# Gated linear and softmax attention: query features turned by VectorE in 32 by 32 blocks, numerators on sixteen tiles of TensorE, value tiles by way of DRAM

## The chip, the cores and the metric

The kernel runs on one core of one Trainium2 chip. The metric is the device time of one execution in microseconds; the median of several runs is given. Engines are named as in the profile: PE (TensorE, with PEld for its weight loads), DVE (VectorE), ACT (ScalarE), POOL (GpSimd), SP (SyncE, which issues most DMAs here). "Line L538" is a line of the kernel before, unless it is said to be of the changed one; the two have other line numbers.

## The reference, cut

Two attentions over the same input, S=2048 tokens, D=448, H=16 heads of Dh=28, mixed by a gate for each token.

```python
def A(x, wqkv, w_phi, wo):                       # hedgehog, linear
    q, k, v = split_heads(x @ wqkv)
    pq = einsum("bhsd,hdf->bhsf", q, w_phi)      # and pk from k
    phi_q = concatenate([softmax(pq), softmax(-pq)], -1)   # 56 features a head; phi_k too
    kv  = einsum("bhsf,bhsd->bhfd", phi_k, v)
    z   = einsum("bhsf->bhf", phi_k)
    num = einsum("bhqf,bhfd->bhqd", phi_q, kv)
    den = einsum("bhqf,bhf->bhq", phi_q, z)[..., None] + 1e-6
    return merge_heads(num / den) @ wo
def B(x, wqkv, wo):                              # softmax attention
    q, k, v = split_heads(x @ wqkv)
    return merge_heads(softmax(q @ k.T * Dh**-0.5) @ v) @ wo
g = sigmoid((x * gate_w).sum(-1, keepdims=True))
return g * A(x) + (1 - g) * B(x)
```

## The kernel before

**Number format.** Projections are made of fp32r products. Weights and x are split into a high and a low part (XH, XL), and a projection of 128 tokens takes, for each of four blocks of rows, two products of XH (with the high and the low part of the weights), and for three of them one of XL: 11 matmuls of 448 columns, called passes here (`tok_major`, L135; `run`, L117).

**Stages.** The text of the kernel is one list of calls, and each engine does its instructions in the order of that list, so the order of the calls sets the order of the work.

1. To 62 us: queries and keys of B (`proj_qk`, tiles pqk), written to DRAM.
2. 62 to 173 us, loop `t`=0..15 over tiles of 128 tokens: the features of A's keys (pk, `features1`, `features2`), A's values (pva, `value_a`), what is left of B's projections, and `kv_add` (L489), which adds two tiles of keys to the sum pkv, as 64 small products on four 128 by 32 tiles of TensorE.
3. 173 to 253 us, loop `q`=0..15: the features of A's queries, then their use. This is what is changed.
4. To 311 us: the rest of A's outputs (poa), with some value tiles of B (pvb, `value_b`, L753); to 335 us the rest of B's values.
5. 335 to 985 us: the attention loop of B (scores st, exponentials p, products pv), then the end.

**One tile of queries.** `tok_major` makes the product pq. ScalarE copies it out of PSUM (pcq, L451). VectorE takes largest and smallest of each head (extq, L453 and L454), GpSimd subtracts (L457; the second half L459, on VectorE for tiles 1 to 10, else on GpSimd), ScalarE takes the exponential in place in one of four feature tiles (feat0 to feat3, L462), VectorE sums and inverts (fsumq, L469 and L470), GpSimd multiplies (L471). The exponentials stand in a list, `exps`; `take_exps(1)` issues all but the newest, so one is left pending until the next tile. `turn` (L525) then transposes the tile on TensorE, in eight 128 by 128 transposes into PSUM tiles pft (L535), which ScalarE copies to SBUF as fT (L538). For each two tiles, `numer` (L541) multiplies fT by KV, the sum of the keys, in 32 products of 256 columns on eight 64 by 32 tiles (pn, L549).

**Behind a numerator.** `normalize1` copies it out (oU) and sends the row of denominators through DRAM, `normalize2` adds and inverts them on VectorE (dena, L418, L419) and sends them out again, `normalize3` multiplies (L430), `normalize4` splits into high and low part (oTa, L438, L439). `out_a` (L593) multiplies by wo in 12 passes (poa), `out_a2` multiplies by the gate on ScalarE (ga, L601) and stores.

**Units.** The softmax of B needs a bound of each row's maximum. It is made in 56 small pieces that are placed wherever there is room, called units (`mx_unit`, L269): four matmuls of 28 rows into two tiles of two banks each (pmb, pmd, L295), a relu of pmd on ScalarE (rl, L298), and two reductions over pmb and rl on VectorE (L300). `tick` calls a unit between two passes when a count of passes has come to the next number of a list, `pace["at"]`. In stage 2 a unit stands at the start of every second tile, and one or two more by `tick`; in stage 3 and 4 one to each tile from q=11 on.

**PSUM.** Eight banks: before q=20, three for the single-bank tiles (`ps_s`), among them pq, pft, pn and poa, four for pmb and pmd, one for pkv. From q=2 on, every fourth `ps_s` tile takes pkv's place (`turn4`). At q=20 the pool is closed and opened again with another split (`psn`).

## Time and profile before

| | |
|---|---|
| median of 3 runs | 1003.8 us (1003.21 to 1003.91) |
| the profiled execution's own time | 1003.26 us |
| its span | 1001.5 us |
| instructions | 18001 |
| PE busy | 994.9 us (99%) |
| ACT busy | 807.8 us (81%) |
| DVE busy | 659.8 us (66%) |
| POOL busy | 240.0 us (24%) |

Busy times are over the whole span. A timeline row gives the start in microseconds from the span's start, the length, the engine, the line, the operation, the tile written and the tiles read, and how many instructions the row holds; behind it, in brackets, a wait and its releaser. Matmuls are pipelined, so a row's own length overlaps the next one's, and prices are read from start to start. A row of the groups gives the line, the engine, the operation, the count, the busy time and the mean in ns, and then the idle time before them with what ended it.

### The profile page before, as it was taken

What the parts mean: (1) busy time and instruction counts of PE and PEld (TensorE: products, weight loads), DVE (VectorE), ACT (ScalarE), POOL (GpSimd) and SP (SyncE); (2) the same over time, 40 slices, a digit from 0 to 9 for tenths busy, and PEclk for the clock granted to TensorE, in tenths of its full rate; (3) what the DMA queues carried; (4) which work ended last, traced back from release to release, by engine and by line L of the source; (5) the groups of instructions that cost most, each with busy time, mean ns of one, the idle gap of its engine ahead of it and who ended that gap; (6) DMA issues with size and microseconds to landing.
All of it is one profiled execution on the core that took longest, in us unless ns stands there. A gap on an engine that the chain in (4) does not pass through costs nothing.

```text
span 1001.5 us, 18001 instructions
## 1 busy us (share of the span) xinstructions
PE 994.9 (99%) x6472; PEld 557.7 (56%) x6472; DVE 659.8 (66%) x1335; ACT 807.8 (81%) x1532; POOL 240.0 (24%) x222
## 2 busy tenths in 40 slices
PE   9999999999999999999999999999999999999998
PEld 8878878888777533333333333333334444455656
DVE  6467676887645588888888788888886544444202
ACT  5445555567855899999999999999999999979672
POOL 1265455678625211110120100102011011101010
PEclk9999999999999999999999999999999999999999
DMA  8977312312235832332525324443233264216231
GB/s 290 313 238 218 104 66 76 146 46 80 91 114 129 174 87 54 88 82 70 108 58 105 81 51 141 88 101 94 59 88 75 66 125 117 53 38 147 64 105 56
DMA packets 68353, 107.28 MB, mean 107 GB/s; under 512 B 18520, under 2 KB 28424, under 8 KB 68264
## 3 DMA queue, kind: packets, MB, share of 16 engines
q1 hardware_dynamic: 68264, 106.13, 39.0%
q8 instruction: 51, 0.84, 0.4%
q14 instruction: 38, 0.31, 0.1%
HBM read 73.44 MB, written 31.45 MB: 105 GB/s over the span
## 4 chain that ended last, share of the span: by engine, by line
PE 99%; DVE 0%; ACT 0%; issue 0%; POOL 0%; POOLq 0%; ACTq 0%
PE st L991 28%; PE pv L1092 25%; PE pm L332 9%; PE pqk L117 6%; PE poa L117 4%; PE pva L135 4%; PE pk L135 4%; PE pq L117 4%; PE pob L117 3%; PE pmb L295 2%; PE pvb L135 2%; PE pft L535 2%; PE pvb L117 1%; PE pqk L688 1%; PE pn L549 1%; PE pkv L489 1%
## 5 line engine op out<-in xcount | busy, mean ns | idle before, releaser
L994 ACT ACTIVATE p<-st 128x512 f32<-128x512 f32 x1020 | 527.9, 642 | 25.8 <-PE st L991 25.7
L343 DVE TENSOR_REDUCE part<-pm 128x1 f32<-128x512 f32 x450 | 287.6, 686 | 151.1 <-PE pm L332 151.1
L991 PE MATMUL st<-qst,kst 128*128 128x512 f32 x1020 | 301.3, 423 | 0.8 <-ACT vb L753 0.5
L1092 PE MATMUL pv<-p,vb 128*32 128x512 f32 x2048 | 263.6, 602 | 0.0
L991 PEld LDWEIGHTS st<-qst,kst 128*128 128x128 f32 x1020 | 168.8, 188 | 100.1 <-ACT p L994 45.0
L336 ACT ACTIVATE rl<-pm 128x512 f32<-128x512 f32 x200 | 124.7, 624 | 14.6 <-PE pm L332 13.0
L332 PEld LDWEIGHTS pm<-kc,qc 28*128 28x128 f32 x800 | 38.3, 181 | 167.7 <-issue 100.6
L430 POOL TENSOR_TENSOR oUb<-oUb,rsb 128x512 f32<-128x512 f32 x15 | 19.3, 1286 | 459.3 <-DMA rsb<-rdb 332.5
L340 DVE CUSTOM_DVE_ANT_0 rl<-pm,rl 128x512 f32<-128x512 f32 x150 | 102.2, 681 | 0.0
L332 PE MATMUL pm<-kc,qc 28*128 28x512 f32 x800 | 101.2, 495 | 0.0
L1092 PEld LDWEIGHTS pv<-p,vb 128*32 128x32 f32 x2048 | 47.4, 108 | 95.4 <-issue 88.7
L300 DVE CUSTOM_DVE_ANT_0 rl<-pmb,rl 128x512 f32<-128x512 f32 x112 | 72.1, 681 | 40.4 <-ACT rl L298 40.3
L298 ACT ACTIVATE rl<-pmd 128x1024 f32<-128x1024 f32 x56 | 57.6, 1028 | 17.0 <-PE pmd L295 9.4
L117 PE MATMUL pqk<-XH,wB 128*128 128x512 f32 x192 | 59.3, 397 | 0.0
L625 ACT CAST ev<-pqk 128x512 fp32r<-128x512 f32 x28 | 16.1, 588 | 37.9 <-PE pqk L117 28.8
L117 PE MATMUL poa<-woA_s,oTa 128*128 128x448 f32 x180 | 40.7, 375 | 0.0
L117 PEld LDWEIGHTS pqk<-XH,wB 128*128 128x128 f32 x192 | 35.4, 188 | 8.5 <-issue 1.5
L1107 DVE SCALAR_TENSOR_TENSOR acc<-pob,gate,acc 128x448 f32<-128x448 f32 x12 | 8.2, 681 | 47.1 <-PE pob L117 47.1
L135 PE MATMUL pva<-wvA_s,XH 128*128 128x450 f32 x128 | 38.6, 375 | 0.0
L135 PE MATMUL pk<-wkA_s,XH 128*128 128x448 f32 x128 | 37.5, 374 | 0.0
L626 DVE TENSOR_TENSOR ev<-pqk,ev 128x512 fp32r<-128x512 f32 x28 | 19.0, 690 | 28.0 <-ACT ev L625 27.9
L117 PE MATMUL pq<-wqA_s,XH 128*128 128x448 f32 x128 | 37.3, 374 | 0.0
(172 smaller groups left out, 1163.3 us busy)
## 6 DMA issues: line engine op xcount, KB each, us to landing
qkd<-ev SPq DMA_DIRECT2D x28, 512.0 KB
qst<-qkd SPq DMA_DIRECT2D x64, 224.0 KB
kst<-qkd SPq DMA_DIRECT2D x64, 224.0 KB
od<-oTb SPq DMA_DIRECT2D x48, 112.0 KB
rsa<-rda SPq DMA_DIRECT2D x8, 512.0 KB
rsb<-rdb SPq DMA_DIRECT2D x15, 256.0 KB
kc<-qkd SPq DMA_DIRECT2D x64, 56.0 KB
gad<-ga SPq DMA_DIRECT2D x16, 224.0 KB
```

Source lines behind the costliest of these rows:

```text
L117: nc.tensor.matmul(dst, l, r, start=i == 0, stop=i == len(todo) - 1)
L135: nc.tensor.matmul(dst[:, :n], l, r, start=i == 0, stop=i == len(todo) - 1, skip_group_check=True)
L295: nc.tensor.matmul((pb if j < 2 else pd)[:, j % 2, :], qc[js, qt * P:(qt + 1) * P], kc[js, :], start=True, stop=True, tile_position=(32 * ...
L298: nc.scalar.activation(rl, pd, AF.Relu)
L300: nc.vector.tensor_tensor_reduce(rl[:, i, :], pb[:, i, :], rl[:, i, :], 1.0, LOWEST, ALU.add, ALU.max, part[:, col + i:col + i + 1])
L332: nc.tensor.matmul(pm[j], mxs[("qc", gq)][js, qt * P:(qt + 1) * P], mxs[("kc", g, kb)][js, :], start=True, stop=True, tile_position=(32 * ...
L336: nc.scalar.activation(rl, pm[kb], AF.Relu if kb < 3 else AF.Copy)
L340: nc.vector.tensor_tensor_reduce(r, pm[j], r, 1.0, LOWEST, ALU.add, ALU.max, part[:, col + j:col + j + 1])
L343: nc.vector.tensor_reduce(part[:, col + j:col + j + 1], pm[j], AX.X, ALU.max)
L991: nc.tensor.matmul(st, kst_of[(gq // NQ, kt // 4)][:, j, (kt % 4) * P:(kt % 4 + 1) * P], qst_of[gq][:, j, :], start=True, stop=True)
L994: nc.scalar.activation(p, st, AF.Exp, scale=SCALE)
L1092: nc.tensor.matmul(pv[32 * j:32 * j + 32, :], vb[kt // 8][:, kt % 8, 4 * g + j, :], pt[j], start=kt == 0, stop=kt == NT - 1, tile_position ...
```

## The change

1. **Feature tiles.** A tile of features is [128, 32, 32] instead of [128, 16, 64]: each half head has 28 features and four zeros of its own.
2. **`turn`.** One VectorE transpose of 1024 columns, which turns each block of 32 by 32 by itself, instead of eight TensorE transposes and the copies out of PSUM. Four tiles make one fT.
3. **`numer`.** Over four tiles of tokens at once, 128 products of 128 columns on sixteen 32 by 32 tiles, each sum made of two (b=0, 1). Four numerators instead of eight. Since a block is turned by itself, row block a of the array holds tokens 32a to 32a+31 of each of the four tiles, so the outputs, the gate and `ga_d` are laid out anew: `out_a(n, a)` is for the 128 tokens of row block a, the gate goes through DRAM into that order (`g_d`, z_s), and `load_acc` reads in four DMAs.
4. **KV** has eight blocks instead of four, from eight transposes (`kv_out`).
5. **Engines.** The second subtraction of `features1` is on GpSimd for all queries; `normalize1` copies two tiles at once; the first low part of `normalize4` is on VectorE. No exponential of a query is left pending.
6. **Values of B.** Ten value tiles (`EARLY`) instead of three are made in stage 3 (one at q=17), stored to `v_d` in DRAM and loaded later (`load_early`).
7. **Units.** 30 in stage 2, by `tick` every 418/30 passes; one each at q=0 and 1; none from q=2 to 18; 20 from q=19 on, by `tick` within the passes, with a list of four SBUF buffers (`rls`).
8. **PSUM and SBUF.** The pool is closed and opened again at q=4 instead of q=20. The first stacks of the attention loop (qst0, kst0) take wqA's place and are loaded from q=21.

The same functions and the loop, cut to what differs most:

```diff
 def features1(pp, nm, eng):
-        nc.gpsimd.tensor_sub(f[:, :, :DH], pc,
+        nc.gpsimd.tensor_sub(f[:, 0::2, :DH], pc,
                              ext[:, 0, :].unsqueeze(2).to_broadcast([P, H, DH]))
-        eng.tensor_sub(f[:, :, DH:2 * DH],
+        eng.tensor_sub(f[:, 1::2, :DH],
                        ext[:, 1, :].unsqueeze(2).to_broadcast([P, H, DH]), pc)
...
 def turn(u):
-        for a, b, p in zip(cut, cut[1:], pt):
-            for n in range(a, b):
-                nc.tensor.transpose(p[:, (n - a) * P:(n - a + 1) * P],
-                                    f[:, n * P:(n + 1) * P], ident)
-        for a, b, p in zip(cut, cut[1:], pt):
-            nc.scalar.copy(fT_of[tb][:, a:b, tl * P:(tl + 1) * P],
-                           p[:, :(b - a) * P].rearrange("p (n q) -> p n q", q=P))
+        if u % 4 == 0:
+            fT_of[u // 4] = ta.tile([P, 4, 2 * H, 32], F32, tag="fT", name=f"fT{u // 4}", bufs=1)
+        nc.vector.transpose(fT_of[u // 4][:, u % 4].rearrange("p h t -> p (h t)"),
+                            fq.pop(u).rearrange("p h f -> p (h f)"))
...
 def numer(n):
-        for gp in range(2):
-            for r in range(2):
-                for c in range(4):
-                    nc.tensor.matmul(pn[r][32 * c:32 * c + 32, gp * 256:gp * 256 + 256],
-                                     KV[rows, 32 * h:32 * h + 32], fT_of[tb][rows, n, :],
-                                     start=True, stop=True, tile_position=(64 * r, 32 * c),
-                                     skip_group_check=True)
-        num[tb] = normalize1(ta, pn, f"a{tb}", 2)
+        pn = [ps_mx(f"pn{n}_{i}", False) for i in range(2)] if n else pn_next
+        for g in range(NG):
+            for b in range(2):
+                for a in range(4):
+                    for c in range(4):
+                        rows, k = slice(32 * a, 32 * a + DH), 2 * g + b
+                        nc.tensor.matmul(pn[a // 2][32 * c:32 * c + 32, a % 2, g * P:(g + 1) * P],
+                                         KV[rows, k // 4, k % 4 * P + 32 * c:k % 4 * P + 32 * c + 32],
+                                         fT_of[n][rows, :, 2 * (4 * g + c) + b, :],
+                                         start=b == 0, stop=b == 1, tile_position=(32 * a, 32 * c),
+                                         skip_group_check=True)
...
 stage 2, for t in range(NT):
-        if t < NT and t % 2 == 0:
-            mx_unit()
-            passes = (55 if t < NT - 4 else 44) + (4 if t >= 4 else 0)
-            pace["n"] = 4 if t >= 4 else 0
-            pace["at"] = [passes // 3, 2 * passes // 3] if t <= 10 else [passes // 2]
+    pace.update(n=0, at=[j * 418 // 30 for j in range(30)])       # once, ahead of the loop
...
 stages 3 and 4, for q in range(NT + 11):
+    VALUE = {2: 0, 3: 1, 4: 2, 5: 3, 6: 4, 7: 5, 8: 6, 9: 8, 10: 9, 17: 10, 22: 7}
+        if q == NT + 3:
+            pace.update(n=0, at=[14, 21, 27, 43, 50, 65, 72, 79, 86, 93, 100, 106, 112, 118, 124, 130, 136, 141, 146, 150])
+        for u in ((), (q - 3, q - 2), (q - 2,), (q - 2,))[(q - 2) % 4]:
+            if 0 <= u < NT:
+                turn(u)
...
+        if q in VALUE:
+            value_b(VALUE[q], tick if q > NT + 2 else None)
...
+        take_exps()
+        if q % 4 == 2 and 6 <= q <= NT + 2:
+            numer(n4)
```

What stands on TensorE before, in the query stage behind the product of tile 11 (pq11) and ahead of that of tile 12: a unit (pmb28, pmd28), the numerator of tiles 6 and 7 (pn3), an output (poa0) and the turn of tile 8 (pft8).

```order
L295 MATMUL pmb28_2543<-kp0_3_750,qp1_1_907 128x512 x2
L295 MATMUL pmd28_2544<-kp0_3_750,qp1_1_907 128x512 x2
L549 MATMUL pn3_0_2553<-fT3_2449,KV_2053 32x256 x4
L549 MATMUL pn3_1_2554<-fT3_2449,KV_2053 32x256 x4
L549 MATMUL pn3_0_2553<-fT3_2449,KV_2053 32x256 x4
L549 MATMUL pn3_1_2554<-fT3_2449,KV_2053 32x256 x4
L117 MATMUL poa0_2583<-woA_s_1874,oTa0_0_2494 128x448 x6
L117 MATMUL poa0_2583<-woA_s_1874,oTa0_1_2497 128x448 x6
L535 MATMUL pft8_0_2600<-ident_76,feat0_464 128x128 x4
L535 MATMUL pft8_4_2601<-ident_76,feat0_464 128x128 x4
```

And of the changed kernel, from the last passes of pq14 on: an output, and the first rows of the numerator of tiles 8 to 11 (pn2), which reads the third fT.

```order
L116 MATMUL pq14_2966<-wqA_s_661,XL_94 128x448
L116 MATMUL pq14_2966<-wqA_s_661,XH_93 128x448 x2
L116 MATMUL poa0_3_2995<-woA_s_1947,oTa0_1_1_2842 128x448 x12
L552 MATMUL pn2_0_3012<-fT2_2849,KV_2131 32x128 x8
L552 MATMUL pn2_1_3013<-fT2_2849,KV_2131 32x128 x8
L552 MATMUL pn2_0_3012<-fT2_2849,KV_2131 32x128 x8
L552 MATMUL pn2_1_3013<-fT2_2849,KV_2131 32x128 x8
L552 MATMUL pn2_0_3012<-fT2_2849,KV_2131 32x128 x8
```

Units and turns are gone from TensorE here, and a numerator alternates between its two PSUM tiles, eight products at a time, 16 such rows in all.

What stands on ScalarE before, from the exponential of tile 9 (feat1) to that of tile 10 (feat2), with the copy of tile 11's product between them (pcq11).

```order
L462 ACTIVATE feat1_465<-feat1_465 128x16x56
L538 COPY fT3_2449<-pft7_0_2505 128x4x128
L538 COPY fT3_2449<-pft7_4_2506 128x4x128
L451 COPY pcq11_2536<-pq11_2524 128x448
L298 ACTIVATE rl28_2549<-pmd28_2544 128x1024
L409 COPY oUa3_2571<-pn3_0_2553 128x512
L409 COPY oUa3_2571<-pn3_1_2554 128x512
L462 ACTIVATE feat2_466<-feat2_466 128x16x56
```

And of the changed kernel, from the last copy of a numerator (oUa1_1) to the copy of tile 12's product; feat3 holds tile 11.

```order
L413 COPY oUa1_1_2814<-pn1_1_2680 128x1024
L458 COPY pcq11_2832<-pq11_2820 128x448
L444 CAST oTa0_1_0_2839<-oUa0_1_2490 128x512
L444 CAST oTa0_1_1_2842<-oUa0_1_2490 128x512
L593 ACTIVATE ga0_0_2865<-poa0_0_2852,z_s_84 128x448
L469 ACTIVATE feat3_470<-feat3_470 128x32x28
L458 COPY pcq12_2895<-pq12_2883 128x448
```

The exponential of a tile now stands ahead of the copy of the next tile's product; before, it stood behind it, with the copies of turn and unit between.

What stands on VectorE before, from the extremes of tile 11 to the product of the normalisation (L430).

```order
L453 TENSOR_REDUCE extq11_2538<-pcq11_2536 128x16
L454 TENSOR_REDUCE extq11_2538<-pcq11_2536 128x16
L300 ISA rl28_2549,part_94<-pmb28_2543,rl28_2549 128x512
L300 ISA part_94 128x1
L300 ISA rl28_2549,part_94<-pmb28_2543,rl28_2549 128x512
L300 ISA part_94 128x1
L469 TENSOR_REDUCE fsumq10_2578<-feat2_466 128x32
L470 RECIPROCAL fsumq10_2578<-fsumq10_2578 128x32
L430 TENSOR_TENSOR oUa1_2307<-oUa1_2307,rsa1_2383 128x1024
```

And of the changed kernel, from the extremes of tile 11 to the first of tile 12.

```order
L460 TENSOR_REDUCE extq11_2834<-pcq11_2832 128x16
L461 TENSOR_REDUCE extq11_2834<-pcq11_2832 128x16
L445 TENSOR_TENSOR oTa0_1_0_2839<-oUa0_1_2490,oTa0_1_0_2839 128x512
L476 TENSOR_REDUCE fsumq10_2845<-feat2_469 128x32
L477 RECIPROCAL fsumq10_2845<-fsumq10_2845 128x32
L541 STREAM_TRANSPOSE fT2_2849<-feat0_467 128x1024
L541 STREAM_TRANSPOSE fT2_2849<-feat1_468 128x1024
L424 TENSOR_SCALAR dena1_0_2811<-dena1_0_2811 128x32
L425 RECIPROCAL dena1_0_2811<-dena1_0_2811 128x32
L424 TENSOR_SCALAR dena1_1_2816<-dena1_1_2816 128x32
L425 RECIPROCAL dena1_1_2816<-dena1_1_2816 128x32
L460 TENSOR_REDUCE extq12_2897<-pcq12_2895 128x16
```

The two reductions of a unit are gone from here, and two transposes of 1024 columns, a low part (L445) and two pairs for the denominators have come, all ahead of the extremes of tile 12.

405 lines of the change are left out of this document (207 added, 198 removed).

## The prediction

> **What bounds the kernel now.** I read the page first: how much of the span TensorE fills, and what the chain that ended last is made of.
>
> ```profile
> span 1001.5 us, 18001 instructions
> PE 994.9 (99%) x6472; PEld 557.7 (56%) x6472; DVE 659.8 (66%) x1335; ACT 807.8 (81%) x1532; POOL 240.0 (24%) x222
> PE 99%; DVE 0%; ACT 0%; issue 0%; POOL 0%; POOLq 0%; ACTq 0%
> q8 instruction: 51, 0.84, 0.4%
> ```
>
> The chain is TensorE from end to end. A busy TensorE may still be a slow one, so the second view is the table by stretches, cut at the stages: keys and A's values (62 to 173 us), query features (to 253), the tail of A (to 311), B's last values (to 335), and the attention loop behind them.
>
> ```profile
> 62.00:173.00 111.00, 111.00 (x946) 90.73 (x949) 76.71 (x168) 60.44 (x99) 58.18 (x51) 1.00 0.38 122
> 173.00:253.00 80.00, 80.00 (x690) 67.09 (x678) 65.34 (x115) 52.89 (x90) 58.54 (x48) 1.00 0.28 98
> ...
> 335.00:985.00 650.00, 649.16 (x3992) 278.11 (x3991) 432.88 (x869) 609.61 (x1221) 67.61 (x64) 1.00 0.36 87
> ```
>
> After stretch and length stand PE, PEld, DVE, ACT and POOL, then the granted clock (1.00 throughout). The change ends before 335, so the loop behind it keeps its time. In the query stage VectorE is busy 65.3 of 80 us and GpSimd 58.5: there is slack, but not much. Third, who made TensorE wait in the front, from the list of waits, and the one such place in the timeline:
>
> ```profile
> PE pqk L671 <- POOL ident masks.py:199: 1.4, 1, 1.4
> PE pmb L295 <- ACT vb L753: 0.6, 1, 0.6
> PE st L991 <- ACT vb L753: 0.5, 1, 0.5
> 279.96 0.50 PE L295 MATMUL pmb<-kp,qp 28*128 28x512 f32 x2 [0.62 <-ACT vb L753]
> ```
>
> 2.5 us in all. So the front is a sum of TensorE's instructions, and what the change takes off that sum is gained unless it makes TensorE wait.
>
> **TensorE's sum.** The timeline of TensorE gives prices from start to start:
>
> ```profile
> 122.04 0.99 PE L489 MATMUL pkv<-feat,vap 128*32 128x56 f32 x64
> 122.97 0.68 PE L135 MATMUL pk<-wkA_s,XH 128*128 128x448 f32 x2
> ...
> 216.41 1.09 PE L549 MATMUL pn<-fT,KV 56*32 56x256 f32 x32
> 217.44 1.09 PE L535 MATMUL pft<-ident,feat 128*128 128x128 f32 x8
> 218.29 0.64 PE L117 MATMUL pq<-wqA_s,XH 128*128 128x448 f32 x2
> ...
> 222.82 1.04 PE L535 MATMUL pft<-ident,feat 128*128 128x128 f32 x8
> 223.61 0.65 PE L117 MATMUL pq<-wqA_s,XH 128*128 128x448 f32 x2
> ...
> 300.93 0.50 PE L295 MATMUL pmb<-kp,qp 28*128 28x512 f32 x2
> 301.37 2.71 PE L117 MATMUL poa<-woA_s,oTa 128*128 128x448 f32 x12
> 304.00 0.50 PE L295 MATMUL pmb<-kp,qp 28*128 28x512 f32 x2
> ```
>
> - *Turns.* By the code 16 turns of eight transposes. A turn takes 0.85 us behind other tile shapes (217.44 to 218.29) and 0.79 behind passes (222.82 to 223.61). Removed: 12.6 to 13.6 us, taken as **-13.4**. ScalarE's copies of them out of PSUM go too.
> - *Numerators.* Before, eight of 1.03 us (216.41 to 217.44): 8.2 us. Each is 32 records on eight tiles side by side, so four rounds of 256 columns; a kv update is 64 records on four tiles, 16 rounds of 56, in 0.93 us (122.04 to 122.97). With c per column and a fixed f, 1024c+f=1.03 and 896c+f=0.93 give c=0.78 ns, f=0.23 us. After, a numerator is 128 products, 256 records on sixteen tiles: 16 rounds of 128, 2048c+f=1.83 us, if records can be issued that fast. If instead the records set the pace, at the kv update's 14.5 ns each, it is 3.7 us. No row shows sixteen tiles. I take 2.2, near the column price that two rows agree on: four of them, 8.8 us, **+0.6** on balance (-0.9 to +6.6).
> - *kvT.* Eight transposes instead of four, 0.1 us each: **+0.4**.
> - *Units moved.* All 56 are still there. From 300.93 to 304.00 is one unit with 12 passes: 3.07 us. From 218.29 to 222.82, 22 passes take 4.53, 0.206 each, so a unit among passes costs 3.07-2.47=0.60, of which 0.44 (300.93 to 301.37) are its own and the rest two changes of tile shape. Eleven units stood beside a numerator or kv update and shared a change; now none does: some +1.1. The turns' lead-ins vanish, 16 times about 0.07 (two passes in 0.48 instead of 0.41): -1.1. **0**.
>
> TensorE's sum falls by 12.4 us. [...] No run here shows sixteen tiles.
>
> **What TensorE may now wait for.** Rows for the other engines:
>
> ```profile
> 136.00 0.50 PE L295 MATMUL pmb<-kp,qp 28*128 28x512 f32 x2
> 136.60 1.02 ACT L298 ACTIVATE rl<-pmd 128x1024 f32<-128x1024 f32 x1
> 137.66 0.69 DVE L300 CUSTOM_DVE_ANT_0 rl<-pmb,rl 128x512 f32<-128x512 f32 x1 [0.25 <-ACT rl L298]
> 138.28 0.69 DVE L300 CUSTOM_DVE_ANT_0 rl<-pmb,rl 128x512 f32<-128x512 f32 x1
> ...
> L469 DVE TENSOR_REDUCE fsumq<-feat 128x32 f32<-128x896 f32 x12 | 13.0, 1080 | 5.4 <-ACT feat L462 5.4
> L459 DVE TENSOR_TENSOR feat<-extq,pcq 128x448 f32<-128x448 f32 x9 | 9.6, 1065 | 0.9
> L454 DVE TENSOR_REDUCE extq<-pcq 128x16 f32<-128x448 f32 x13 | 7.9, 606 | 0.0
> L470 DVE RECIPROCAL fsumq<-fsumq 128x32 f32<-128x32 f32 x12 | 4.2, 353 | 0.4
> L430 DVE TENSOR_TENSOR oUa<-oUa,rsa 128x1024 f32<-128x1024 f32 x3 | 3.5, 1161 | 0.0
> L418 DVE TENSOR_SCALAR dena<-dena 128x32 f32<-128x32 f32 x5 | 2.5, 490 | 0.0
> L263 DVE STREAM_TRANSPOSE nm<-red 128x32 f32<-128x32 f32 x1 | 0.2, 213 | 0.0
> L471 POOL TENSOR_TENSOR feat<-feat,fsumq 128x896 f32<-128x896 f32 x16 | 30.3, 1896 | 20.9 <-DVE fsumq L470 15.9 <-ACT pcq L451 2.6 <-DVE dena L418 1.8
> L457 POOL TENSOR_TENSOR feat<-pcq,extq 128x448 f32<-128x448 f32 x16 | 18.2, 1135 | 1.7 <-DVE extq L453 1.7
> L462 ACT ACTIVATE feat<-feat 128x896 f32<-128x896 f32 x32 | 30.7, 959 | 1.1 <-POOL feat L457 0.8 <-POOL feat L459 0.3
> ```
>
> - *Key stage.* 30 units now stand 14 passes apart: 14 x 0.206 + 0.60 = 3.5 us. A unit's second bank comes free when VectorE is done with the unit ahead, 2.97 us after that one's start (136.00 to 138.97). Behind it VectorE does two extremes, a sum and a reciprocal (0.6+0.6+1.08+0.35=2.6 us), which pushes the next unit's reductions to 2.97+2.6+1.3=6.9, and the unit after that comes at 7.0. So it just fits, or is late by some 0.2 us once per two tiles: 0 to 13 us (30 times 0.45, if each is delayed to the limit), taken as **+1.0**.
> - *Query stage, VectorE.* A transpose of 1024 columns: 213 ns for 32, and 1.06 ns per further element by L454 and L469 ((1080-606)/448), is 1.26 us; by the slowest row per element (L459, 2.4 ns, with GpSimd beside it) 2.6. I take 1.26, the same class of one-input work. For four query tiles VectorE then has features 4 x 2.6, transposes 5.0, and per numerator two reciprocal pairs 1.7, two products 2.3, two subtractions 1.4 (0.69 each, a unit's row being as long): 20.8 us. TensorE has 4 x 23 passes and a numerator: 18.9+2.2=21.1. VectorE fits by a hair, and unevenly: a tile with two turns and the reciprocals takes 7.5 us against TensorE's 4.7.
> - *Query stage, the loop.* ScalarE now runs tile q's exp before the copy of tile q+1's product; before, one exp was always left pending. Copy, extremes, GpSimd's subtractions (1.14+0.95), exp (0.96): 0.55+0.65+2.1+0.96, 4.3 us with no slack beyond 4.5 to 4.7. When VectorE is 2.3 or 2.8 us late (behind tiles 7 and 11), the copy of the tile behind is too, and with two banks left in that rotation TensorE waits: 0.55 and 0.65 us. Behind tile 15 the last sum, product and two transposes end 13.0 us after its product, TensorE's work until the last numerator 12.1: 0.9; and the third group's first output follows 0.6 late. **+2.7** (0 to 9, the latter if each of sixteen tiles takes half a microsecond longer).
> - *Tail.* 20 units at 4 to 7 passes, on three PSUM buffers and four in SBUF. The last five stand 1.5 us apart against 0.6+1.02 for ScalarE's step: **+0.5** (0 to 2). The ten early value tiles go to DRAM and back on SP, ahead of their use by 100 us; nothing on TensorE waits for them: 0.
> - *A wait gone.* The change of PSUM pools, where the 0.62 us stood, moves to a quiet place: **-0.6** (0 if it only moves).
>
> Sum: -12.4+1.0+2.7+0.5-0.6 = -8.8. The profiled execution took 1003.26 us (1.8 around its span); 1003.26-8.8=994.5. The median of the runs lies 0.5 above that execution, so the forecast is **995.0 us**, with 990 to 1001 for this case alone.
>
> **Rivals.**
> - *All of it is hidden (0.25).* The waits above don't come, as each is under a microsecond and the queues have elastic ends: -12.4-0.6, 990.8. For it: TensorE waited 2.5 us in the front of a kernel whose query stage was 82% VectorE. Against: the stage is now near 100%.
> - *VectorE becomes the bound of the query stage (0.13); this one ends slower.* The one unseen VectorE instruction is the 1024-column transpose. Each 0.1 us above 1.26 costs 16 x 0.1, as VectorE has no slack left there. The gain is gone at 1.26+8.8/16=1.8 us, and it is slower by over 0.2% from 1.94. At twice the price per element (2.3 us) it is 995.0+16.6, about 1012. For it: only a 32-column transpose is in the trace. Against: all one-input rows have 1.06 ns.
> - *The numerators starve (0.17).* At 14.5 ns per record they cost 6 us more: 1001.0. A second reason leads to the same place: 51 instruction packets serve 12,944 records of PE and PEld, 254 each, and took 0.4% of 16 engines' span, 1.26 us each; a numerator of 256 products and as many loads eats one in about 0.9 us, two in a row. Waits of 0.4 to 1.5 us each would be 1.6 to 6. [...]
>
> **How the numbers follow.** Forecast 0.45, hidden 0.25, starving 0.17, VectorE 0.13. The range reaches from below the hidden case (988, if the turns' lead-ins count for more) to past the starving one (1004.5), and leaves out the VectorE case and a little below. What a measurement can tell from no change is 0.2%, 2 us: faster means under 1001.8. Faster: 0.44 of the forecast, all of hidden, 0.09 of starving, 0.78. Same: 0.07. Slower: VectorE's 0.13 and 0.02 of starving, 0.15.
>
> **What would show it.** Right: no pft rows; numerators of about 2 us from start to start, four of them; STREAM_TRANSPOSE of 1024 columns at about 1.26 us; in the query stage waits of TensorE below 1 us each, put down to ScalarE's copies, and one before the last numerator; the loop behind starting some 9 us earlier and as long as before. Wrong: transposes above 1.8 us, numerators above 3, or waits of the units in the key stage that sum to over 5 us.

## The result, and the profile after

| | before | after |
|---|---|---|
| median of four runs | 1003.5 us (1003.2 to 1003.9) | 1033.6 us (1032.4 to 1035.5) |
| ratio | | 1.0301 (1.0283 to 1.0319) |
| span of the profiled execution | 1001.5 us | 1031.1 us |

The change makes the kernel 3.0% slower; the forecast was 0.9% faster. First from the page of the profile of the changed kernel: the span, the engines' busy times and what the chain that ended last is made of.

```profile
span 1031.1 us, 19220 instructions
PE 1003.3 (97%) x7116; PEld 563.5 (55%) x7116; DVE 679.2 (66%) x1349; ACT 794.6 (77%) x1491; POOL 236.6 (23%) x230
PE 92%; DMA 5%; DVE 2%; issue 1%; SPq 0%; ACT 0%; POOL 0%; POOLq 0%; DVEq 0%; ACTq 0%
```

The chain was all TensorE and is now 8% other things. The table by the same stretches as before (length, PE, PEld, DVE, ACT, POOL, then the granted clock):

```profile
62.00:173.00 111.00, 111.00 (x926) 86.20 (x924) 80.92 (x186) 65.38 (x101) 53.98 (x46) 1.00 0.36 116
173.00:253.00 80.00, 76.20 (x953) 66.55 (x952) 55.74 (x93) 35.92 (x56) 50.39 (x53) 0.96 0.31 105
253.00:311.00 58.00, 47.63 (x690) 40.43 (x688) 40.15 (x53) 23.68 (x35) 32.13 (x25) 0.90 0.24 81
311.00:335.00 24.00, 17.16 (x66) 12.71 (x63) 9.17 (x23) 7.86 (x11) 2.57 (x3) 0.75 0.59 146
```

Three things are to be seen: the key stage is as full as before, TensorE has idle time from 173 us on, and the clock, 1.00 everywhere before, falls below 1 in just those rows. By the first product of the attention loop (pv) the loop starts at 365.1 us instead of 336.2, **28.9 us later**, and from there to the end it takes 666.0 us instead of 665.3. So the loss lies wholly ahead of the loop: 6.3 us in the key stage (eight more units), 13.2 from the first product of the queries to the last numerator, 9.4 from there to the loop. The list of what TensorE waited for, up to 380 us, its four largest entries:

```profile
PE pmd L295 <- ACT rl_s L302: 7.6, 3, 6.3
PE pn L552 <- issue: 6.9, 4, 2.6
PE pmb L295 <- DVE part L304: 4.3, 1, 4.3
PE poa L116 <- ACT oTa L444: 2.9, 1, 2.9
```

21.7 us, in few and long pieces, where the same stretch before had 1.1 (the 1.4 of pqk at the start is unchanged). The places follow one by one. TensorE's fp32 products stand in the trace as two records each (1024 for the 512 of four numerators); what the text ahead of the prediction calls the 32 products of a numerator and the 64 of a kv update before are records, of 16 and 32 products.

**A numerator, and the clock behind it.** TensorE's timeline at the first numerator (tiles 0 to 3), then the clock in two stretches behind it:

```profile
215.28 3.01 PE L552 MATMUL pn<-fT,KV 28*32 28x128 f32 x206
219.51 0.94 PE L552 MATMUL pn<-fT,KV 28*32 28x128 f32 x50 [1.23 <-issue]
220.38 1.07 PE L116 MATMUL pq<-wqA_s,XH 128*128 128x448 f32 x2
...
221.63 0.95 PE L116 MATMUL pq<-wqA_s,XH 128*128 128x448 f32 x2
222.37 0.58 PE L116 MATMUL pq<-wqA_s,XL 128*128 128x448 f32 x1
```

```profile
220.00:224.00 4.00, 4.00 (x32) 3.42 (x27) 0.00 (x0) 1.93 (x2) 0.00 (x0) 0.57 0.07 13
224.00:228.00 4.00, 4.00 (x22) 3.71 (x21) 2.87 (x5) 1.39 (x3) 2.14 (x3) 1.00 0.04 4
```

From start to start the numerator takes 5.10 us (215.28 to 220.38), its siblings 6.41, 5.34 and 5.70: 22.6 in all. 6.9 of them are the waits put down to issue: the profile shows nothing that TensorE waited for. The queue of the instructions has one packet of 16 KB between 217.0 and 218.1 us and none from 218.2 to 219.4, in the middle of this numerator. In all four numerators the wait ends 1.2 to 1.5 us after such a packet has landed, so I read it as a wait for instructions. The row is that of the queue from 217.0 to 218.1 us.

```profile
q8 instruction: 1, 0.02, 5.5%
```

Without the waits a numerator takes 3.9 us, 15.6 for four. The products themselves come at 14.5 ns per record (206 in about 3.0 us), 29 ns per product, which is the pace of a kv update before.

Then, behind each numerator, passes take 0.37 us instead of 0.205 (221.63 to 222.37 is two of them), and the granted clock is 0.57 for these four microseconds and 1.00 again in the next four. I counted the passes that start 0.36 to 0.6 us apart up to the loop: 24 up to the last numerator, 34 behind it, none before the change; what they take beyond 0.205 sums to 4.3 and 6.3 us, the latter 7.0 with the units that stand among them, together **11.3 us**. The lists of waits don't show this term.

**The tail.** The two longest pieces of the chain that ended last (start, length, what), and then the instructions that lead to TensorE's two longest waits in this stretch, with the two products that waited as the last lines:

```profile
286.85 12.95 DMA rsa<-rda
...
314.73 16.36 DMA qk<-nm
```

```profile
302.34 4.77 DVE L424 TENSOR_SCALAR dena<-dena 128x32 f32<-128x32 f32 x1
302.30 1.29 POOL L445 TENSOR_TENSOR oTa<-oUa,oTa 128x512 fp32r<-128x512 f32 x1 [2.93 <-ACT oTa L444]
303.52 3.55 POOL L873 MEMSET qk<- 128x2048 f32 x2
322.42 1.23 DVE L436 TENSOR_TENSOR oUa<-oUa,rsa 128x1024 f32<-128x1024 f32 x1 [8.63 <-DMA rsa<-rda]
323.68 1.14 ACT L444 CAST oTa<-oUa 128x512 fp32r<-128x512 f32 x2 [7.93 <-DVE oUa L436]
324.73 1.01 ACT L302 ACTIVATE rl_s<-pmd 128x1024 f32<-128x1024 f32 x1
310.57 0.80 PE L295 MATMUL pmb<-kp,qp 28*128 28x512 f32 x2 [4.32 <-DVE part L304]
325.80 0.79 PE L295 MATMUL pmd<-kp,qp 28*128 28x512 f32 x2 [6.33 <-ACT rl_s L302]
```

The normalisation of a numerator is a chain of copy, denominators to DRAM and back, sum and reciprocal, reciprocals to DRAM and back as a broadcast over the partitions (rsa), product, cast and low part. For the last two numerators it takes 23 and 32 us from the start of the copy to the first output (273.3 to 296.7 us, 297.6 to 329.9); before, the last one took 30 (274.5 to 304.4). The two broadcasts for tiles 8 to 11 take 8.7 us (286.03 to 294.75) and 12.95; the first for tiles 12 to 15, issued at 311.10, lands at 322.40. For that one VectorE's product (L436) waits until 322.42, ScalarE's cast waits for that product until 323.68, the relu of a unit (L302) stands behind the cast in ScalarE's queue, and the unit's next product on TensorE waits for the relu: 6.3 us. The last chain also starts late: the copy of the last numerator stands on ScalarE behind the cast of the one ahead, which waits for its own broadcast, and begins at 297.60, 3.9 us after the numerator has ended. The second long piece, the load of the bounds for the loop's first stacks (qk<-nm), is taken up in experiment 3.

The 4.3-us wait is of another kind: VectorE's add to 32 columns (L424) takes 0.12 to 0.18 us where GpSimd is idle. Here it takes 4.77 us, and the unit's reductions that TensorE waits for stand behind it. It lies beside a low part on GpSimd and the clearing of the loop's first stacks, and ends (307.11) with that clearing (303.52+3.55=307.07); the next add (307.42, 1.55 us) ends with the third clearing. The ends fall together within 0.04 us, and the 4.77 us span three instructions of GpSimd.

### The profile page after: what moved, and what is told of

Its sections match the earlier page's. It is cut to its first block, busy times and chain, and to the rows that moved or that the text cites. A ratio compares the mean times of both kernels' runs of the same rounds, so it can differ in the third digit from the quotient of the medians.

```text
span 1031.1 us, 19220 instructions
## 1 busy us (share of the span) xinstructions
PE 1003.3 (97%) x7116; PEld 563.5 (55%) x7116; DVE 679.2 (66%) x1349; ACT 794.6 (77%) x1491; POOL 236.6 (23%) x230
## 4 chain that ended last, share of the span: by engine, by line
PE 92%; DMA 5%; DVE 2%; issue 1%; SPq 0%; ACT 0%; POOL 0%; POOLq 0%; DVEq 0%; ACTq 0%
PE st L1009 27%; PE pv L1108 24%; PE pm L336 8%; PE pqk L116 6%; PE pq L116 4%; PE pk L135 4%; PE pva L135 4%; PE pob L116 3%; PE pmb L295 2%; PE pvb L116 2%; PE poa L116 2%; DMA qk<-nm 2%; DMA rsa<-rda 1%; PE pvb L135 1%; PE pn L552 1%; DMA kst<-qkd 1%
## 5 line engine op out<-in xcount | busy, mean ns | idle before, releaser
L436 POOL TENSOR_TENSOR oUb<-oUb,rsb 128x512 f32<-128x512 f32 x15 | 19.3, 1287 | 460.2 <-DMA rsb<-rdb 196.3
L1009 PE MATMUL st<-qk,kst 128*128 128x512 f32 x384 | 116.2, 425 | 0.6 <-DMA kst<-qkd 0.6
L1009 PE MATMUL st<-qst,kst 128*128 128x512 f32 x384 | 114.8, 423 | 0.0
L1009 PEld LDWEIGHTS st<-qst,kst 128*128 128x128 f32 x384 | 64.3, 188 | 37.8 <-ACT p L1012 16.5
L1009 PEld LDWEIGHTS st<-qk,kst 128*128 128x128 f32 x384 | 63.9, 188 | 38.6 <-ACT p L1012 17.8
L304 DVE CUSTOM_DVE_ANT_0 rl<-pmb,rl 128x512 f32<-128x512 f32 x88 | 56.5, 679 | 27.0 <-ACT rl L302 26.9
L302 ACT ACTIVATE rl<-pmd 128x1024 f32<-128x1024 f32 x44 | 45.2, 1027 | 28.6 <-PE pmd L295 20.1
L116 PE MATMUL poa<-woA_s,oTa 128*128 128x448 f32 x192 | 48.9, 407 | 2.9 <-ACT oTa L444 2.9
L116 PEld LDWEIGHTS poa<-woA_s,oTa 128*128 128x128 f32 x192 | 39.7, 212 | 9.7 <-ACT oTa L444 3.2
L469 ACT ACTIVATE feat<-feat 128x896 f32<-128x896 f32 x32 | 30.6, 956 | 13.5 <-POOL feat L466 13.5
L116 PE MATMUL pq<-wqA_s,XH 128*128 128x448 f32 x128 | 39.9, 395 | 0.0
```

The lines of the kernel that those rows point to most:

```text
L116: nc.tensor.matmul(dst, l, r, start=i == 0, stop=i == len(todo) - 1, skip_group_check=mid is not None)
L302: nc.scalar.activation(rl, pd, AF.Relu)
L304: nc.vector.tensor_tensor_reduce(rl[:, i, :], pb[:, i, :], rl[:, i, :], 1.0, LOWEST, ALU.add, ALU.max, part[:, col + i:col + i + 1])
L469: exps.append(lambda: nc.scalar.activation(fx, fx, AF.Exp))
L1009: nc.tensor.matmul(st, kst_of[(gq // NQ, kt // 4)][:, j, (kt % 4) * P:(kt % 4 + 1) * P], qst_of[gq][:, j, :], start=True, stop=True)
```

## The experiments

Ratios are to the kernel before, run on the same chip, with their 95% intervals; waits are those of the list up to 380 us where nothing else is said. "Idle" is the time in which TensorE has no instruction, counted up to the last product of the last numerator and from there to the loop; after the change these are 6.9 and 14.9 us.

**1. What a numerator costs: its instruction packets, its records, its columns.** In the first, a numerator is issued in four parts with three passes between them; in the second it has 64 products of 256 columns, in the third 64 of 128. The second and third leave out or replace part of the products, so their numerators have other values.

```diff
+ numer(n4, [g])            # g = 0, 1, 2 behind passes 2, 5, 8 of the value or output
- numer(n4)
+ numer(n4, [3])
```

> Each numerator is cut into four parts of 32 products, with three passes of a value or output product between one part and the next; nothing is left out. Theory A (records set the pace of a numerator at 14.5 ns each, the wait inside it is for its instructions, and the clock falls because a stretch of some 3 us holds little else): the passes between give the instructions time to come, the waits put down to issue (6.9 us in the four numerators) fall under 2 us, and no pass behind a numerator takes 0.37 us any more (about 5 us over the four); four parts pay three more changes of tile shape, 0.6 us a numerator. Time 1022 to 1026. Theory B (sixteen tiles don't run side by side, cost goes by columns, and the wait is for data): the waits stay where the data are late, the sum of the parts stays at 3.7 us, and the time stays within 3 us of 1033.6. In both the waits of the units in the tail (10.6 us) stay.

Measured 1028.4 us, 1.0251 (1.0236 to 1.0267): 5.2 us less than after. It is 2.4 us above what theory A gave. The timeline of one part:

```profile
219.71 1.07 PE L554 MATMUL pn<-fT,KV 28*32 28x128 f32 x64
```

The next pass starts at 220.71, so a part takes 1.00 us and the records keep their pace, 15.6 ns here; all 6.9 us of issue waits are gone. 4.0 came back in two new waits of pn for fT, because a numerator that begins earlier waits for its last transposes. The loss to the half clock up to the last numerator fell from 4.3 to 2.0 us, all of it behind the longer of these waits (3.2 us).

```diff
-        for g in range(NG):
+        for g in (0, 2):
...
-                        nc.tensor.matmul(pn[a // 2][32 * c:32 * c + 32, a % 2, g * P:(g + 1) * P],
+                        nc.tensor.matmul(pn[a // 2][32 * c:32 * c + 32, a % 2, g * P:(g + 2) * P],
```

> Each numerator has 64 products of 256 columns instead of 128 of 128: half the records, the same columns. The columns of one more block of features are multiplied in place of another's, so the numerators' values change. Theory A (records at 14.5 ns): 128 records, 1.9 us a numerator, at most a short wait for instructions, no half clock behind it: some 3.7 us a numerator and 5 us of clock less in all, time 1012 to 1018. Theory B (columns): a numerator stays at 3.7 us or more without its wait, time above 1024.

```diff
-            for b in range(2):
+            for b in range(1):
```

> Each numerator has only its first 64 products (b=0) of 128 columns: half the records and half the columns; the second half of the features is left out of the numerators. Theory A: as long as with 64 products of 256 columns, within 0.3 us a numerator (1.9 us), time 1012 to 1018. Theory B: half as long as those, 1 us, and 4 us less in time over the four.

Measured 1025.5 (1.0226, 1.0209 to 1.0242) and 1025.0 us (1.0210, 1.0186 to 1.0234). Theory A had both at 1012 to 1018. They miss it because waits came in their place: for ScalarE's copies and the transposes 4.8 and 5.8 us in the query stage, and the wait behind the last numerator grew from 2.9 us to 5.4 and 6.4. One numerator of each, and the clock of each kernel in the query stage:

```profile
215.88 2.76 PE L552 MATMUL pn<-fT,KV 28*32 28x256 f32 x128
```

```profile
216.09 1.91 PE L552 MATMUL pn<-fT,KV 28*32 28x128 f32 x128
```

```profile
173.00:253.00 80.00, 79.42 (x735) 68.02 (x734) 61.07 (x103) 39.40 (x60) 54.30 (x56) 1.00 0.32 107
```

```profile
173.00:253.00 80.00, 78.55 (x738) 68.24 (x739) 61.85 (x104) 39.37 (x60) 55.14 (x56) 1.00 0.32 107
```

A record of 128 columns costs 14.9 ns, about as one of 56 columns in the kv update before (14.5); one of 256 columns costs 21.5. So at 128 columns the count of records sets the price, and only at 256 do the columns show. Half the records in one burst give no issue wait either.

The clock stays at 1.00 up to the last numerator in both. The second kernel has bursts nearly as long as after the change (2.76 us) and no wait in them. The third is idle for 6.6 us up to there, about as much as after (6.9), and its pieces (0.8 to 1.7 us) are as long as two of the four after (1.2 and 1.35), but they stand between whole passes or ahead of a short numerator. So neither a burst of 2.76 us alone nor idle pieces up to 1.7 us halved the clock in these two; after the change it was halved, up to the last numerator, behind waits of 1.2, 2.6 and 1.35 us that stand within a burst. The other three halvings after the change came in waits of 2.9 us, right behind the last numerator, and of 4.3 and 6.3 us in the tail.

**2. Two parts instead of four.**

```diff
+ mid = (lambda i: i == 4 and numer(n4, [0, 1])) if q in (6, 10, 14, 18) else None
...
- numer(n4)
+ numer(n4, [2, 3])
```

> Each numerator in two parts of 64 products with seven passes between them, nothing else; nothing is left out. If a block of 256 instructions needs some 2.7 us to come, 256 instructions of a part and the gap now last 3.3 us, and the waits put down to issue go as they did with four parts; two tile changes fewer a numerator save 0.5 us each: 1025.5 to 1028. If a part of 256 instructions is still too much at a time, waits of 0.5 to 1 us stay in each numerator: 1028 to 1031.

Measured 1026.6, 1.0228 (1.0212 to 1.0243). The second part of the first numerator, and the issue waits in the list:

```profile
217.24 1.90 PE L554 MATMUL pn<-fT,KV 28*32 28x128 f32 x128
219.07 0.68 PE L116 MATMUL pq<-wqA_s,XH 128*128 128x448 f32 x2
219.78 0.57 PE L116 MATMUL pq<-wqA_s,XH 128*128 128x448 f32 x2
```

```profile
PE pn L554 <- issue: 0.6, 1, 0.6
```

Of 6.9 us of issue waits 0.6 are left, and the passes behind run at full clock (219.07 to 219.78 is three, with the change of tile shape in it). A row of 256 instructions now lasts 1.8 us, with seven passes behind it. The numerator's own price stays 2 x 1.83. Only the last numerator, behind a wait of 3.0 us for fT, still has the half clock (1.9 us). This change of order is worth 7 us, and it is as far as the query stage came.

**3. The tail: clearing and loads.** The clearing of the stacks and their loads go behind the early values.

```diff
-        if q == 21:
+    # behind vb.append(value_tile(1))
     for i in range(2):
         nc.gpsimd.memset(w[:, i], 0.0)
     ...
     load_q(0); load_nm(0); load_k(0, 0)
```

> The first stacks of the attention loop are cleared and loaded behind the last output of A instead of at q=21; nothing is left out. Theory C (the tail waits because the chain of the last numerators, through DRAM and back, takes over 20 us, and the value tiles that stood there have been made before): the waits for units and outputs in the tail keep their sum (14 us and the half clock behind them) within 4 us, and the loads may add a wait of some us ahead of the first scores: 1030 to 1037. Theory D (the early loads hold up SP's queue, where the four issues of load_nm take 13.2 us, and the clearing on GpSimd holds up VectorE, whose addition to dena took 4.8 us instead of 0.5): the waits of 4.3 and 6.3 us go, with the half clock behind them: 1016 to 1022.

Measured 1030.1, 1.0263 (1.0246 to 1.0281): 3.5 us less. Two entries of the list, and the add of 32 columns that had taken 4.77 with the GpSimd instruction beside it:

```profile
PE pmd L295 <- ACT rl_s L302: 7.5, 1, 7.5
...
PE st L959 <- POOL vb L760: 4.4, 1, 4.4
```

```profile
300.57 1.28 DVE L424 TENSOR_SCALAR dena<-dena 128x32 f32<-128x32 f32 x1
300.53 1.28 POOL L445 TENSOR_TENSOR oTa<-oUa,oTa 128x512 fp32r<-128x512 f32 x1 [3.01 <-ACT oTa L444]
```

The 4.3-us wait of pmb is gone; the wait for the broadcast (7.5) is not, and the broadcast takes 9.7 us (305.38 to 315.08) without the loads beside it, 11.3 with them: the loads are not what makes it long. The loop's first scores now wait 4.4 us for what came late. The short add again lasts as long as the GpSimd instruction beside it.

**4. The tail: order.** The calls behind the query stage are written out by hand in another order, so that the chain of the last numerators starts earlier and has value tiles beside it; two versions of it, and both with numerators in two parts.

```diff
- EARLY = (0, 1, 2, 3, 4, 5, 6, 8, 9, 10)
+ EARLY = (0, 1, 2, 3, 4, 5, 6, 8, 9, 10, 11, 12, 13, 14)
+    value_b(7, tick); norm4b(2, 0)
+    num[3, 1] = normalize1(ta, pn_of[3][1], "a3_1", 2)      # the second copy, later
+    out_a(2, 0)
+    # then normalize2 of numerator 3, load_early, value tile 11, norm4b(2, 1), outputs, loads ...
```

> The tail alone is put in another order; nothing is left out. The value tiles 11 to 14 go by way of DRAM too and stand, with tile 7, between the outputs of tiles 8 to 11, so that some 100 passes and 12 units stand between the last numerator and the outputs that need it; the multiplication and the low parts of the last numerator, and the casts of the one ahead, stand later on VectorE's and ScalarE's queues; the first stacks are cleared on VectorE before the last numerator and loaded behind the last numerator's transfers. Theory C (the tail waits for the chain of the last numerators through DRAM, 22 to 31 us, with the units' relus and reductions queued behind it): the waits of 2.95, 4.3 and 6.3 us go to under 4 in sum, and with them some 6 us of half clock behind them; time 1014 to 1019. Theory E (the transfers are slow for want of bandwidth, and whatever stands behind the last numerator waits for them): the same sum of waits at other places, above 1026. The waits and half clock of the numerators (12 us) stay in both.

Measured 1038.2, 1.0348 (1.0329 to 1.0368), 4.6 us worse, where theory C had 1014 to 1019. From the chain that ended last:

```profile
313.35 10.64 DMA rda<-dena
...
324.06 9.27 DMA rsa<-rda
```

With the two copies apart, the second store of reciprocals, a small one, is issued behind the load of the early values (vb<-vd, 1.8 MB, issued at 310.36) and the first broadcast (512 KB, 312.13) on the same queue, and lands after 10.6 us instead of 1.9. The chain got longer, 37 us, and the loop, loaded late, took 672.3 us.

> The tail in its new order and the numerators in two parts, with seven passes between the parts; nothing is left out. If the two causes (instructions of the numerators, chain of the tail) are all of it and add up, the front has the changed kernel's sum of work, 365.1 less 21.8 us of waits and 12.7 of half clock, 330.6, and 2 to 5 us for parts and small waits: the loop starts at 333 to 336 us against 336.2 before, time 999 to 1004. If something else holds the query stage once these are gone (VectorE, 20.8 of each 21 us by the prediction's sum), waits for the copies of pq grow to over 1 us a tile and the time is 1006 to 1014.

Measured 1032.1, 1.0288 (1.0273 to 1.0304): the two parts bring 6.1 us here as they brought 7.0 alone, so the two stages add up. Neither 999 to 1004 nor 1006 to 1014 was reached, since the tail kept its waits (12.5 us idle).

```diff
- EARLY = (0, 1, 2, 3, 4, 5, 6, 8, 9, 10)
+ EARLY = (0, 1, 2, 3, 4, 5, 6, 8, 9, 10, 11, 12)
+    # both copies of numerator 3 at once, then:
+    normalize2(3); value_b(7); norm4b(2, 0); out_a(2, 0); value_b(11); norm4b(2, 1); out_a(2, 1)
+    value_b(12); out_a(2, 2); normalize3(3, 0); out_a(2, 3); norm4b(3, 0); normalize3(3, 1)
+    load_early(0); load_q(0); load_nm(0); load_k(0, 0); out_a(3, 0); norm4b(3, 1); out_a(3, 1..3)
```

> The numerators in two parts, and the tail in a second order; nothing is left out. Against the first reordering, both halves of the last numerator are copied out at once (the second into a part of the last fT's place), so that both broadcasts of the reciprocals start together; only tiles 11 and 12 are made ahead of the last outputs beside tile 7, 13 to 15 stay behind, where the other stacks are cleared; the first stacks are cleared by GpSimd behind the last transpose and loaded behind the last numerator's transfers. Theory C (the chain of the last numerators is what the tail waits for; the first reordering failed because it cut that chain in two and made it 37 us long, and because the loop's first loads came late): waits in the tail under 5 us, no wait for kc in the loop, time 1003 to 1011. Theory E (whatever stands there waits, since the transfers keep ScalarE's, VectorE's and SP's queues blocked in turn): the tail's waits stay at 11 to 14 us in sum, 1020 to 1028.

Measured 1024.2, 1.0211 (1.0193 to 1.0230): 9.4 us less than after, the shortest of those that leave nothing out, and far from the 1003 to 1011 of theory C. The tail is idle for 9.2 us instead of 14.9, and the loop takes 668.4 us, 3 more than before. What is left in the list:

```profile
PE poa L116 <- DVE oTa L445: 6.4, 1, 6.4
PE pn L554 <- DVE fT L541: 3.3, 2, 3.0
```

The 6.4 stands where normalize2 of the last numerator, waiting for its denominators, has the low part of the one before behind it on VectorE. The obvious repair is to exchange the two:

```diff
-    for i in range(2):
-        num[3, i] = normalize2(ta, *num[3, i], f"a3_{i}", 2, True)
     value_b(7, tick)
     norm4b(2, 0)
+    for i in range(2):
+        num[3, i] = normalize2(ta, *num[3, i], f"a3_{i}", 2, True)
```

> As the second reordering of the tail with numerators in two parts (1024.2 us), but the sum and reciprocal of the last denominators stand on VectorE behind the low part of the numerator ahead, not ahead of it; nothing is left out. There the low part, and with it TensorE (6.4 us), waited for a transfer of the last numerator. Theory I (a place in VectorE's queue alone): that wait goes, the last chain starts up to 2 us later: 1017 to 1021. Theory J (the stretch is bound by the chain of transfers, so that a wait taken away comes back behind it): the waits of the tail keep their sum within 2 us, 1022 to 1026.

Measured 1024.4, 1.0216 (1.0201 to 1.0232), no difference. The wait fell and others took its place, as theory J had it; the loop takes 670.0 us:

```profile
PE poa L116 <- DVE oTa L445: 3.6, 1, 3.6
...
PE pmd L295 <- ACT rl_s L302: 2.5, 2, 2.2
PE pm L336 <- DMA kc<-qkd: 2.4, 2, 1.4
```

**5. The tail: what covers the chain.** In the first kernel the tail's 20 units go to its end; in the second three value tiles, made early by the change, are made in the tail again.

```diff
- pace.update(n=0, at=[14, 21, 27, 43, ...])
+ pace.update(n=0, at=[])
```

> The 20 units of the tail are taken out of it and stand in one row behind the last value tile, ahead of the loop; nothing is left out. The time itself will be longer, since a row of units goes at the pace of ScalarE or VectorE, 1.4 to 2 us each, 16 to 28 us more. What it shows is the tail without units. Theory C (chain): TensorE then waits for oTa of the last numerator itself, 8 to 14 us in one piece, and some 3 to 5 us for that of the numerator ahead. Theory F (the units bring the waits: too dense for ScalarE and VectorE): the tail is then free of waits, under 3 us in sum.

Measured 1065.8, 1.0629 (1.0612 to 1.0647). Two entries of the list from 290 to 400 us, and the instruction on ScalarE behind the longer wait:

```profile
PE poa L116 <- ACT ga L593: 16.0, 2, 11.4
PE pmb L295 <- DVE part L304: 10.2, 18, 0.8
```

```profile
319.82 1.14 ACT L444 CAST oTa<-oUa 128x512 fp32r<-128x512 f32 x2 [13.72 <-DVE oUa L436]
```

The 11.4 us end at 321.54, when ga, which stands behind this cast on ScalarE, has emptied a PSUM tile; the cast has waited 13.7 us for the product, and that for the broadcast. So without units between them, the outputs show the wait of the chain bare, in one piece, and 20 units in a row cost 10.2 of their own. By the mean granted clocks (0.966 of 1060.5 us, 0.984 of 1031.1 after) I estimate some 40 us more at half clock than after. The units of the tail are not the cause of its waits; they were covering some of it.

```diff
- VALUE = {... 8: 6, 9: 8, 10: 9, 17: 10, 22: 7}
+ VALUE = {... 8: 6, 18: 8, 19: 9, 20: 10, 22: 7}
```

> Three value tiles are moved from the query stage (q=9, 10, 17) to q=18, 19 and 20; nothing is left out. Theory C: 6.8 us of work stand where the chains of the last two numerators are waited for: the wait for the outputs of tiles 8 to 11 (2.95 us) goes, the waits of the units fall by 3 to 6 us, and the half clock behind one of them goes; the query stage takes it back only where VectorE is the bound, 0 to 4 us: 1025 to 1031. Theory F: the waits of the units stay, 1032 to 1036.

Measured 1026.5, 1.0235 (1.0214 to 1.0257), 7.1 us less, by moving TensorE's work of three tiles. What the tail still waits for:

```profile
PE pmd L295 <- ACT rl_s L302: 3.3, 2, 3.1
PE poa L116 <- ACT ga L593: 2.9, 1, 2.9
```

The tail's idle time fell from 14.9 to 7.4 us, the query stage's rose from 6.9 to 10.1 (2.6 of it a new wait of a numerator for fT). The value tiles were the cover.

**6. The transposes and numerators alone.** Units, values and stacks stand as in the kernel before; numerators in two parts. In the second kernel three value tiles more are early.

```diff
- EARLY = (0, 1, 2, 3, 4, 5, 6, 8, 9, 10)
+ EARLY = (0, 1, 2)                          # second kernel: 0 to 5
+ VALUE = {8: 0, 9: 1, 10: 2, 18: 3, 19: 4, 20: 5, 21: 6, 22: 7}
+ numer(n4, [0, 1]) behind tile q; numer(n4, [2, 3]) behind pass 8 of the next
```

> The core of the change alone: features turned by VectorE and numerators on sixteen tiles, these in two parts with eight passes between. The units, the value tiles and the first stacks go back to their places in the kernel before (21 units in the key stage, one to each tile of queries from q=11; three value tiles at q=8 to 10 by way of DRAM, five at q=18 to 22, eight behind; stacks ahead of those eight). Nothing is left out. Theory G (the moved units and values brought the tail's loss, since the work that covered the last numerators' chain went into the query stage): the tail's waits stay under 5 us, the query stage waits 8 to 20 us in all, for VectorE and ScalarE, as the turns that filled TensorE there are gone: 1008 to 1022, below any other version with the turns on VectorE. Theory H (the chain of four tiles is the cause, wherever units and values stand): the tail waits 8 us or more again, 1022 to 1032. A query stage that is a third idle without a half clock would show how much idling the clock stands.

> As the core alone, but six value tiles instead of three are made in the query stage (q=3 to 6, 8, 9) and stored, two at q=19 and 21, eight behind. Nothing is left out. Theory G: three tiles, 6.8 us, fill waits of the query stage and are missed in the tail only for the part by which the chain is then uncovered: 2 to 6 us under the core alone. Theory H: the same time within 2 us, what the query stage gains the tail loses.

Measured 1037.7 (1.0340, 1.0322 to 1.0358) and 1037.0 us (1.0329, 1.0312 to 1.0347). The first lies above what either theory gave; the second has the same time within 2 us, as theory H had it. The list of the first, and a stretch of its query stage:

```profile
PE pn L554 <- DVE part L304: 10.7, 2, 7.1
PE pn L554 <- DVE fT L541: 6.3, 1, 6.3
```

```profile
200.00:220.00 20.00, 13.31 (x289) 10.86 (x289) 11.64 (x18) 7.12 (x10) 12.48 (x12) 0.74 0.03 5
```

In the first the tail is idle for only 2.6 us now, but the query stage for 23.8, and in the second for 5.8 and 19.4: with fewer value tiles in the query stage, TensorE runs ahead of the transposes and of the PSUM tiles that it shares with the units, and VectorE is busy 11.6 of 20 us while it is waited for. So the moves of values and units are not by themselves what makes the change slow; the work can be put where either the one or the other stage starves, and the turns, which filled TensorE in the query stage before, are no longer there.

**7. VectorE's slack.** Each transpose is done twice.

```diff
+        for _ in range(2):
             nc.vector.transpose(...)
```

> The changed kernel with each of the 16 transposes on VectorE done twice, the second like the first; nothing is left out. 16 times 1.2 us are added to VectorE. If VectorE has no slack in the query stage, as the prediction's rival took it, the time grows by 15 to 19 us. If it has slack as the stage stands (filled with values, TensorE waiting for instructions), by 0 to 6 us, with new waits for fT ahead of the numerators.

Measured 1043.8, 1.0400 (1.0381 to 1.0419): 10.2 us for 16 more transposes. Their row, and the largest new entry of the list:

```profile
L543 DVE STREAM_TRANSPOSE fT<-feat 128x1024 f32<-128x1024 f32 x32 | 38.6, 1219 | 0.6
```

```profile
PE pn L554 <- DVE fT L543: 6.7, 4, 3.9
```

16 x 1.22 is 19.6 us of VectorE's time, and half of it reached the end. That lies between what either side expected: VectorE has slack in the stage, but not at the numerators, which wait for the last transposes.

## Why the prediction was wrong, step by step

- *The turns, right in size.* No pft rows are left, and VectorE's transposes are as priced, 1.19 us against 1.26:

```profile
L541 DVE STREAM_TRANSPOSE fT<-feat 128x1024 f32<-128x1024 f32 x16 | 18.8, 1193 | 0.8 <-POOL feat L478 0.8
```

  The rival that VectorE becomes the bound through a dear transpose is out.
- *The numerators: a mis-sized term.* I took 2.2 us from a column price between two rows, and named the other bound, 14.5 ns per record, as a rival. It is that one: 14.5 ns, 15.6 us for four instead of 8.8. The kv update, 56 columns at 14.5 ns per record, was the row to read: two rows gave two straight lines, and I took the one that made the change pay. Where columns did show (256 of them, experiment 1), 2048 columns took 2.76 us, not the 1.83 of my line. The two records of a product take 29 ns.
- *The instruction packets: the rival's second reason, given as an alternative, came on top.* 6.9 us against "1.6 to 6". The prediction added neither, and 1001.0 took only one.
- *The clock: a term that was missing.* 11.3 us, 4.3 behind the first three numerators and 7.0 from the last one on. The clock was 1.00 in every row before, and I put no term for what a burst with a wait in it, or a long wait, does to it.
- *The tail, "+0.5" and "nothing on TensorE waits for them: 0": a step that failed, with the numerators.* I costed each moved piece at its own place, ten value tiles at zero. What they had hidden, the chain between the last numerator and its outputs, I didn't follow. Before, 62 us of TensorE's work stood in this stretch, twelve value tiles among it; after the change it has six, 13.5 us less, and the chain is as long as it was (30 us before, 32 after). 14.8 us of waits lie in the tail, instead of the 0.5. About 10 of them are for the chain; the other 4.3 come from the add beside the clearing of the first stacks, a moved piece that I gave no term at all. Experiment 5 shows the cover: waits come bare when the units are taken out, and halve when three value tiles are put back. Experiment 6 limits this: with all values back the tail's idle time goes (2.6 us), but the query stage takes it on (23.8).
- *Units: right.* A unit with seven passes of the tail takes 2.06 us from start to start (339.69 to 341.75), so one among passes costs 0.62; I had 0.60.
- *Key stage, "+1.0": right within what can be told.* No wait of the key stage is in the list, and its 6.3 us are eight more units at 0.62 and about one more.
- *Query stage, "+2.7".* The small waits on ScalarE's copies that I summed hardly came in the changed kernel: behind the bursts TensorE was late anyway. They came where the bursts were mended (pq<-pcq 1.2 us in the fastest version), as did the wait before a numerator (3.0 us instead of 0.9).

The account, against the start of the loop that the forecast implied (336.2-8.8=327.4, so 37.7 us too early): numerators' records 6.8, packets 6.9, half clock 11.3, other waits 14.8 where 4.7 were forecast, 10.1 more. That is 35.1; 2.6 us are not accounted for, small idle pieces that no list names among them. The numerators (records, packets and the half clock behind the first three) make 18.0 of it, the tail's waits and half clock 17.1: two failed steps of about the same size.

What stays open: the fastest version still starts its loop 16.6 us after the kernel before, and ends 20.9 later, some 3 us of it in the loop. Its numerators (about 15 us instead of 8.2), waits and half clock, less the turns, make some 12 of the 16.6; the rest isn't placed. Whether another order could make the change pay was not settled: no version came nearer than 2.1%, and the numerators' records alone take back half of what the turns save (15.6-8.2=7.4 of 13.4). Nor is it shown what decides the clock, only when it fell. And no run made the broadcast itself shorter: it takes 9 to 14 us in the chains followed here (after, experiments 3 and 4).

## What to carry to other kernels

Price a change of many small matmuls by the count of instructions as well as by columns, at the slower of the two rows that the trace has, and add a term for long rows of them: 512 instructions in a row waited 1.2 to 2.6 us each time here, 6.9 us in four numerators, and parts of 256 0.6 us in all. When work moves from a full engine's late stage to an early one, look for the long chain (a DRAM round trip, a broadcast) that this work was hiding: its price appears at the place the work left. And a wait on TensorE can cost twice, once as itself and once as half clock behind it: here waits of 1.2 to 2.6 us within a burst of small products did (after), and waits of 2.9 to 3.2 us next to one (after, experiments 1 and 2), while pieces up to 1.7 us between whole passes or ahead of a short burst cost themselves alone (experiment 1, third kernel).

## What the runs showed of the hardware

- After the change each of the four waits put down to issue ends 1.2 to 1.5 us after a packet of 16 KB on the instruction queue has landed, 2.4 to 2.8 us after its transfer began. Rows of 512 instructions at 14.5 ns per record had 6.9 us of such waits in four numerators; rows of 256 in 1.9 us, followed by seven passes, had 0.6 (experiment 2).
- Up to the loop the clock's records after the change have six stretches of half clock, three of 3.41 us and three of 6.83. The first begins 0.95 us behind the end of a wait of 1.2 us in a burst of 32 by 32 products. The clock stayed at 1.00 up to the last numerator with 6.6 us of idle time in pieces up to 1.7 us, and with bursts of 2.76 us without a wait (experiment 1, third and second kernel).
- A small transfer that was issued on a queue behind a load of 1.8 MB and a broadcast of 512 KB landed after 10.6 us instead of 1.9 (experiment 4, first kernel).
- VectorE's add to 128x32 took 0.12 to 0.18 us in the seven of 16 cases, before and after, that had no GpSimd instruction beside them. The other nine ended 0.04 us behind a GpSimd instruction that ran beside them, and so did one in experiment 3: 4.77 us beside three of them, 1.28 beside one.
